# Attention with complex decay and a low-rank mixer on one core: transposed inputs of five pairs by DMA, matmuls of neighbouring chunks joined, a new order

## The chip, the cores and the metric

The kernel runs on one core of a Trainium2 chip. The core has five engines with a queue each: TensorE (PE: matmuls, with the weight loads as PEld), VectorE (DVE), ScalarE (ACT), GpSimd (POOL) and SyncE (SP); the last two issue DMAs here. The metric is device time of one launch in microseconds, the median of several runs. A difference of about 0.2% can be told from none.

## The reference, cut to what matters

B = 4 batches, H = 8 heads, S = 768 tokens, D = 48. Attention is a linear recurrence with a complex gate, whose magnitude is held under 0.999; its real output goes into a mixer over tokens of rank 32 and an MLP over 384 channels. All tensors are f32 for this kernel's purpose, and the order of the sums is free.

```python
mag = np.sqrt(a_re * a_re + a_im * a_im)
scale = np.minimum(mag, 0.999) / (mag + 1e-06)
a_re_n, a_im_n = (a_re * scale, a_im * scale)
for t in range(S):
    new_re = ar * S_re - ai * S_im
    new_im = ar * S_im + ai * S_re
    kv = np.einsum('bhd,bhe->bhde', k[:, :, t], v[:, :, t])
    S_re, S_im = (new_re + kv, new_im)
    y[:, :, t] = np.einsum('bhd,bhde->bhe', q[:, :, t], S_re)
x = attn_out.transpose(0, 2, 1, 3).reshape(B, S, H * D)
u = x + (x.transpose(0, 2, 1) @ U @ V).transpose(0, 2, 1)    # U: 768x32, V: 32x768
out = u + np.maximum(u @ w_ch1, 0.0) @ w_ch2                  # 384x1536, 1536x384
```

## The kernel before

**Chunks.** The 3072 tokens are 24 chunks `i` of 128 (six to a batch), each in two halves of 64. For a chunk, gates are loaded, their magnitudes and angles are summed along the tokens with matmuls against a prefix matrix (L777, L782, L842, L845), and q and k are turned by the gates. q and k are then split into 16-bit halves (ACT, L466), written to DRAM (SP, L933) and read back by a DMA transpose (SP, L934), or transposed on TensorE (L908). `chain(i)` (L938) then does for all heads: the products q*k inside each half (L956, psum "inner"), a masked copy into AT, the state's increments of each half (`state`, L976, into two psum banks `dk`), the states GM and G by additions, what a half adds from inside itself (`inside`, L1005, two psum banks `y`), what comes from before it (`before`, L1013, into the same two banks), and three ScalarE copies out of `y` into `xo` (L1022, L1024).

**Pairs.** `mixer(m)` (L1029) works on pairs of chunks, m = 0 to 11. Once a batch's six chunks are there, `rank` (L1048) forms xU, `spread` (L1071) forms its product with V for each chunk, DVE adds it to `xo` (L472), and `turned` transposes the result: three TensorE transposes a chunk (L1087) into a psum bank and one ScalarE copy to `uT` (L1091). For the first pairs the hidden layer comes from `up` (L1102, L1142) and `down` (L1303); from pair 3 on `up_fewer` makes the first product by a scheme with fewer products: DVE forms twelve combinations of uT's blocks (`put`, L1186), TensorE multiplies them in groups (`few`, L1214, 8 records to a group), ScalarE or a DVE operation makes h, and `down_two` (L1346) forms the second product, which DVE adds to `xo`. The result leaves by DMA from POOL.

**Psum banks.** Kinds "Y" and "T" share five banks, which go round (`psum`): `dk`, `y`, `rank`, `spread`, the transposes, the prefix sums and some of the `few` groups all take the next one. "inner" has its own, `down` and `few` have others.

**Order.** The functions only record operations in a `Plan`, each with its engine, reads, writes and an estimated cost. A table of operation numbers, `ORDER`, sets the sequence in which they are emitted, and so the sequence on every engine's queue; the compiler keeps it. `SPARE` (L1506) and `WARM` (L1513) put idle matmuls at some numbers. `again` (L665) loads the gates once more to find their range and issues one DMA of 192 KB for each chunk and each part (L671).

Of the kernel before, what the change touches and what calls it, by code (L numbers as in the profile page):

```python
# [10 lines left out]
FP = mybir.dt.float32  # L11
I32 = mybir.dt.int32
# [106 lines left out]
)  # L119

SPARE = {
    410: 3, 447: 1,
}

WARM = {
    112: (2, 1), 126: (1,), 136: (2, 2, 2, 2, 2, 2, 1), 141: (2,), 162: (2, 2, 2), 235: (2, 2, 2, 2, 1), 242: (2,), 245: (2,), 259: (2, 2, 1), 266: (1, 1, 1, 1, 1, 1, 1, 1, 1),
}

AIM = {}

DUMP = None

# [194 lines left out]
def kernel(  # L327
# [40 lines left out]
    GROUPS = [(n, n + GC) for n in range(0, NT, GC)]  # L368
    PARTS = [[(n, n + 1) for n in range(GC)]] + [[g] for g in GROUPS[1:]]
    NG = len(GROUPS)  # L370
    AGAIN = range(NG)

    EARLY, SPREAD = 6, (0, 1, 2)
    SPLIT = range(3, NG)
# [563 lines left out]
    def chain(i):  # L938
# [26 lines left out]
        if not last:  # L965
            buffer(G, "G", 2, [DQ, H, D])
# [616 lines left out]
```

## Time and profile before

| | us |
|---|---|
| median of 3 runs | 530.15 (529.94 to 530.81) |
| the profiled execution | 529.77 |
| its span | 528.0 |
| mean granted TensorE clock | 0.997 |
| gate loads on SP, 48 of them `again`'s | 96 of 192.0 KB |
| DMA packets, bytes | 280670, 87.06 MB |

The profile is of one execution. Times of matmuls are of records: a matmul in f32 leaves two records, and a row "x6" of the timeline stands for three matmuls of the code. Records overlap in TensorE's pipeline, so the cost of a group is the distance from its first start to the next group's.

### The profile page before, as it was taken

How to read it: one execution, taken by the hardware profiler on the slowest of the kernel's cores; microseconds unless marked ns; L12 is line 12 of the kernel's file. 1: busy time of each engine (PE TensorE's matmuls, PEld its weight loads, DVE VectorE, ACT ScalarE, POOL GpSimd, SP SyncE). 2: the span in 40 equal slices, each digit the busy share in tenths (PEclk: the TensorE clock that was granted, in tenths of full speed). 3: DMA queues.
4: the chain of work that ended last, by engine and by line, in shares of the span. 5: the costliest groups of instructions: out<-in, count | busy, mean ns of one | idle time of the engine just before them, and what ended most of it. 6: DMA issues, size and time to landing. Idle time of an engine off the chain costs nothing.

```text
span 528.0 us, 15692 instructions
## 1 busy us (share of the span) xinstructions
PE 509.3 (96%) x6670; PEld 460.3 (87%) x6670; DVE 414.5 (79%) x787; ACT 346.0 (66%) x555; POOL 31.6 (6%) x61
## 2 busy tenths in 40 slices
PE   4999999899999999999999999999999999999996
PEld 2777887666998997999999989999999989999996
DVE  4779897799989987898798797878796575958452
ACT  8899998998869978978896768843543313131100
POOL 1000000001010000101011000110000000000110
PEclk9999999999999999999999999999999999999998
DMA  9959958479999998999899958999897543333101
GB/s 226 173 115 270 209 115 191 140 138 217 197 215 244 216 215 145 204 217 202 205 198 227 210 144 175 170 242 229 192 217 178 108 90 61 76 60 61 39 32 35
DMA packets 280670, 87.06 MB, mean 165 GB/s; under 512 B 271288, under 2 KB 272784, under 8 KB 280592
## 3 DMA queue, kind: packets, MB, share of 16 engines
q1 hardware_dynamic: 278384, 81.63, 76.0%
q0 software_dynamic: 2208, 4.35, 2.4%
q8 instruction: 54, 0.88, 0.7%
q14 instruction: 24, 0.20, 0.1%
HBM read 43.03 MB, written 23.63 MB: 126 GB/s over the span
## 4 chain that ended last, share of the span: by engine, by line
PE 88%; ACT 5%; DMA 3%; DVE 2%; issue 1%; SPq 0%; ACTq 0%
PE down L1346 25%; PE few L1214 14%; PE bank L1214 11%; PE up L1102 6%; PE inner L956 4%; PE bank L1013 4%; PE bank L976 4%; PE down L1303 3%; PE bank L1005 2%; DMA gate<-F 2%; PE bank L1071 2%; PE bank L1087 2%; ACT gate L466 1%; PE bank L777 1%; PE bank L782 1%; PE bank L842 1%
## 5 line engine op out<-in xcount | busy, mean ns | idle before, releaser
L466 ACT ACTIVATE gate<-gate 128x768 f32<-128x768 f32 (+2 forms) x85 | 86.1, 1018 | 25.8 <-DMA gate<-in_a_im_dram 14.7
L1346 PE MATMUL down<-w,h 128*128 128x192 f32 x396 | 70.4, 328 | 0.0
L466 ACT ACTIVATE QK<-QKC 128x768 uint16<-128x768 uint16 (+1 forms) x72 | 58.5, 848 | 13.1 <-DVE QKC L469 7.9
L1346 PEld LDWEIGHTS down<-w,h 128*128 128x128 f32 x396 | 64.6, 190 | 1.2 <-issue 0.8
L469 DVE TENSOR_TENSOR QKC<-qk,cs 128x768 f32<-128x768 f32 x48 | 44.9, 952 | 1.0 <-ACT cs L466 0.6
L472 DVE TENSOR_TENSOR xo<-down,xo 128x192 f32<-128x192 f32 (+1 forms) x79 | 29.9, 385 | 14.3 <-PE down L1346 14.1
L1222 ACT COPY h<-few 128x512 f32<-128x512 f32 x35 | 20.2, 583 | 27.8 <-PE few L1214 27.6
L1222 ACT COPY h<-bank 128x512 f32<-128x512 f32 x25 | 14.3, 588 | 36.0 <-PE bank L1214 31.0
L1346 PE MATMUL down<-stage 128*128 128x192 f32 x198 | 37.2, 328 | 0.0
L1102 PE MATMUL up<-uT,w 128*128 128x256 f32 x144 | 33.8, 383 | 0.0
L1346 PEld LDWEIGHTS down<-stage 128*128 128x128 f32 x198 | 32.5, 190 | 0.3 <-issue 0.2
L1102 PEld LDWEIGHTS up<-uT,w 128*128 128x128 f32 x144 | 26.7, 190 | 4.9 <-issue 0.6
L1290 POOL DMA_DIRECT2D out_dram<-xo x32 | 18.5, 590 | 202.9 <-DVE xo L472 164.5
L463 ACT ACT_TABLE_LOAD x22 | 28.2, 1283 | 1.1 <-PEq L1567 0.7
L828 POOL DMA_DIRECT2D gate<-F x15 | 12.0, 797 | 274.7 <-DVE stage L616 86.3
L1226 DVE CUSTOM_DVE_ANT_1 h<-few,h 128x512 f32<-128x512 f32 x31 | 21.0, 686 | 8.8 <-PE few L1214 8.1
L1214 PE MATMUL few<-extra,w 128*128 128x128 f32 x216 | 27.8, 275 | 0.0
L956 PE MATMUL inner<-QK 112*64 112x64 f32 x768 | 27.5, 224 | 0.2 <-DVE AT L959 0.2
L466 ACT ACTIVATE cs<-F 128x384 f32<-128x384 f32 x48 | 24.4, 518 | 3.9 <-DVE F L851 3.7
L956 PEld LDWEIGHTS inner<-QK 112*64 112x64 f32 x768 | 24.5, 138 | 2.4 <-issue 0.8
L1214 PEld LDWEIGHTS few<-extra,w 128*128 128x128 f32 x216 | 26.3, 192 | 0.1
L466 ACT ACTIVATE es<-bank 128x384 f32<-128x384 f32 x44 | 18.4, 502 | 9.2 <-PE bank L777 8.2
(185 smaller groups left out, 1166.8 us busy)
## 6 DMA issues: line engine op xcount, KB each, us to landing
xd<-QK SPq DMA_DIRECT2D x36, 512.0 KB
gate<-in_a_re_dram SPq DMA_DIRECT2D x48, 192.0 KB
gate<-in_a_im_dram SPq DMA_DIRECT2D x48, 192.0 KB
stage<-in_moe_w_ch_dram SPq DMA_DIRECT2D x12, 768.0 KB
qk<-in_q_dram SPq DMA_DIRECT2D x24, 192.0 KB
qk<-in_k_dram SPq DMA_DIRECT2D x24, 192.0 KB
VP<-in_v_dram SPq DMA_DIRECT2D x24, 192.0 KB
out_dram<-xo POOLq DMA_DIRECT2D x12, 192.0 KB, 4.2
```

The lines of the kernel that those rows point to most:

```text
L463: ACT(1.37, rank, lambda: nc.scalar.preload_act_table_set(name), writes=[TABLE])
L466: return nc.scalar.activation(out=o, in_=i, func=f, **kw)
L469: nc.vector.tensor_tensor(out=o, in0=a, in1=b, op=OP.mult)
L472: nc.vector.tensor_tensor(out=o, in0=a, in1=b, op=OP.add)
L956: nc.tensor.matmul(out=get(*ps0)[r:r + HC, h], lhsT=k_of(h, r, HC), rhs=q_of(h, r, HC), start=True, stop=True, tile_position=(0, r))
L976: nc.tensor.matmul(out=get(*dk[r])[x:x + D, h], lhsT=get(*ks)[at, h, x // DP, 0:D], rhs=get(*VPi)[at, h], start=True, stop=True, tile_posi ...
L1013: nc.tensor.matmul(out=get(*y[u])[side(r, u), p], lhsT=q_of(h, r * HC, HC), rhs=get(*(mid_G if r else ("G", i - 1)))[:, h], start=False, s ...
L1102: nc.tensor.matmul(out=get(*ps)[:, e], lhsT=w1[:, f, (ff + e) * 128:(ff + e + 1) * 128], rhs=get(*uT)[:, f], start=(f == 0), stop=(f == KD ...
L1214: nc.tensor.matmul(out=get(*ps)[:, q], lhsT=w()[:, q * 128:(q + 1) * 128], rhs=v[0](), start=(n == 0 and q == 0), stop=True, skip_group_ch ...
L1222: ACT(c_act(n3 * CH) - 0.045, RU, lambda i=i, k=k: nc.scalar.copy(out=at(i, k), in_=get(*ps)), [ps], [o])
L1226: DVE(c_dve(n3 * CH), RU, lambda i=i, k=k: nc.vector._custom_dve(dve_ops.TENSOR_ADD_SAT, out=at(i, k), in0=get(*ps), in1=at(i, k), s0=math ...
L1346: nc.tensor.matmul(out=get(*to)[:, part], lhsT=x(j), rhs=y[:, j], start=(first and j == 0), stop=(j == KH - 1), skip_group_check=not first)
```

## The change

1. For pairs 7 to 11 (`TURNED`) the chunk's input is transposed by DMA: `across` splits the f32 values into 16-bit halves on ScalarE (two instructions, into one tile XU), SP writes them to DRAM (192 KB, tag XV, six buffers) and SP reads them back with a DMA transpose into `uT`. The other pairs keep their TensorE transposes.
2. From chunk 8 on (`JOIN`), except for the first chunk of a batch, the operations of two neighbours are joined: `state` of chunk i (all heads) with `inside` of i-1 as one operation, then the `before`s of i-1 with the products of i as one. The psum banks of i-1's `y` are so taken together with i's `dk`, and the ScalarE copies of i-1 are recorded after the masked copy of i. 14 chunks are joined.
3. `again` loads two chunks of a gate with one DMA, contiguous in memory. The range does not depend on the layout.
4. The transposes take `uT` themselves, where before `spread` depended on it.
5. `ORDER`, `SPARE` and `WARM` are new, made with longer times for instructions. SPARE goes from 4 to 2 matmuls, WARM from 33 to 32 (22 of 256 columns instead of 19, 10 of 128 instead of 14).

The diff without the table of numbers, cut:

```diff
 SPARE = {
-    410: 3, 447: 1,
+    422: 1, 447: 1,
 }
@@
+    JOIN = 8
@@
+    XU = singles.tile([128, 2, DM], U16, name="XU")
@@
+    TURNED = (7, 8, 9, 10, 11)
@@ again
-        for (nm, src), i in ((a, i) for a in ((ar, a_re), (ai, a_im)) for i in range(lo, hi)):
-            SP(c_dma(DM), ("load", 30 + n), lambda nm=nm, src=src, i=i: nc.sync.dma_start(out=get(*nm)[:, i - lo], in_=rows(src, i)),
-               writes=[nm + (i,)])
+        b, c = where(lo)
+        for nm, src in ((ar, a_re), (ai, a_im)):
+            SP(c_dma(W), ("load", 30 + n), lambda nm=nm, src=src: nc.sync.dma_start(
+                out=flat4(nm), in_=src[b, :, c * CH:(c + hi - lo) * CH].rearrange("h t d -> h (t d)").rearrange("h (p m) -> h p m", m=W)), writes=[nm])
@@ chain
+        joined, joins = c > 0 and i >= JOIN, not last and i + 1 >= JOIN
...
+        if joined:
+            p_inside, p_in, p_y, p_befores, p_b, p_leaves, p_rooms, p_takes = pending.pop(i - 1)
+            p_rooms()
+
+            def fused_x():
+                state(0, H)
+                p_inside()
+            PE(1.3, RR, fused_x, [ks, VPi] + p_in, [dk[r] for r in parts_k] + p_y, way=3, steps=4 * H * len(parts_k) + 4 * H,
+               takes=[mid_G] + p_takes)
+            states(True)
+
+            def fused_y():
+                p_befores()
+                products()
+            PE(1.8, RR, fused_y, p_b + [QK], p_y + [ps0], takes=[ATi], way=1, steps=8 * H)
+            states(False)
+            kept()
+            p_leaves()
+        else:
+            PE(0.947, RL, products, [QK], [ps0], takes=[ATi], way=1, steps=4 * H)
+            kept()
+            for h0 in (0, HH):
+                PE(0.443, RR, lambda h0=h0: state(h0), [ks, VPi], [dk[r] + (h0,) for r in parts_k], way=3,
+                   steps=4 * HH * len(parts_k),
+                   takes=[mid_G] + ([] if last else [G]))
+            states(True)
+        if joins:
+            pending[i] = inside, y_in, y, befores, b_in, leaves, rooms, [xi]
+            return
@@ mixer, spread
-            PE(0.76, R0, products, [r, ("V", 0)] + [uT + ("kept",)] * (m >= AHEAD), ps, way=5, steps=8)
+            PE(0.76, R0, products, [r, ("V", 0)], ps, way=5, steps=8)
@@ mixer, turned
+            if m in TURNED:
+                across(cc, i, u)
+                return
...
-            PE(0.33, R0, turn, [u], [tr], steps=KD)
+            PE(0.33, R0, turn, [u], [tr], takes=[uT], steps=KD)
@@
+        def across(cc, i, u):
+            xu, xv = ("xu", i), ("xv", i)
+            ring(xu, "xu", [XU])
+            buffer(xv, "XV", 6, [CH, DM], bass.MemoryType.DRAM)
+            for n in range(2):
+                ACT(c_act(DM), R0, lambda n=n: act(get(*xu)[:, n], get(*u).bitcast(U16).rearrange("p (m n) -> p m n", n=2)[:, :, n], AF.Copy),
+                    [u], [xu + (n,)])
+            SP(0.6, R0, lambda: nc.sync.dma_start(out=get(*xv).bitcast(U16), in_=get(*xu).rearrange("p n m -> p (n m)")), [xu], [xv])
+            SP(0.8, R0, lambda: nc.sync.dma_start_transpose(
+                out=get(*uT).rearrange("p f (c t) -> p f c t", c=MC)[:, :, cc].bitcast(U16),
+                in_=get(*xv).bitcast(U16).rearrange("t (n m) -> (t n) m", n=2)), [xv], [uT + (cc,)])
```

Three places of TensorE's queue. First, `spread` and the transposes of batch 1 (chunks 6 to 11) before, where all of `spread` and two prefix matmuls stand ahead of the transposes:

```order
L1071 MATMUL bank_61<-r,V 128x192
L1071 MATMUL bank_62<-r,V 128x192
L1071 MATMUL bank_61<-r,V 128x192
L1071 MATMUL bank_62<-r,V 128x192
L1071 MATMUL bank_63<-r,V 128x192
L1071 MATMUL bank_64<-r,V 128x192
L1071 MATMUL bank_63<-r,V 128x192
L1071 MATMUL bank_64<-r,V 128x192
L842 MATMUL bank_65<-GS_96,prefix_r 128x384
L842 MATMUL bank_65<-GS_97,prefix_r 128x384
L1087 MATMUL bank_61<-ident,xo 128x128 x3
L1087 MATMUL bank_62<-ident,xo 128x128 x3
```

and now:

```order
L1093 MATMUL bank_63<-xo,UV 32x384 x12
L1116 MATMUL bank_64<-r,V 128x192
L1116 MATMUL bank_65<-r,V 128x192
L1116 MATMUL bank_64<-r,V 128x192
L1116 MATMUL bank_65<-r,V 128x192
L1135 MATMUL bank_61<-ident,xo 128x128 x3
L1135 MATMUL bank_62<-ident,xo 128x128 x3
L1116 MATMUL bank_63<-r,V 128x192
L1116 MATMUL bank_64<-r,V 128x192
L1116 MATMUL bank_63<-r,V 128x192
L1116 MATMUL bank_64<-r,V 128x192
L976 MATMUL bank_65<-VP_118,QKC_106 48x48 x2
```

The transposes of the first pair stand between the two halves of `spread`, right behind the half that they need.

Second, the first join: the end of `state` of chunk 8 and the begin of `inside` of chunk 7, now:

```order
L976 MATMUL bank_62<-VP_120,QKC_108 48x48 x2
L976 MATMUL bank_63<-VP_120,QKC_108 48x48 x2
L976 MATMUL bank_62<-VP_120,QKC_108 48x48 x2
L976 MATMUL bank_63<-VP_120,QKC_108 48x48 x2
L976 MATMUL bank_62<-VP_120,QKC_108 48x48 x2
L976 MATMUL bank_63<-VP_120,QKC_108 48x48 x2
L1000 MATMUL bank_64<-VP_119,AT_123 64x48
L1000 MATMUL bank_65<-VP_119,AT_123 64x48
L1000 MATMUL bank_64<-VP_119,AT_123 64x48
```

(`VP_120` and `QKC_108` are chunk 8's, `VP_119` and `AT_123` chunk 7's.) Before, `inside` and the `before`s of chunk 7 ended ahead of five groups of `down`, and `state` of chunk 8 came behind them:

```order
L1013 MATMUL bank_62<-GM,QK_101 64x48
L1013 MATMUL bank_61<-GM,QK_101 64x48
L1013 MATMUL bank_62<-GM,QK_101 64x48
L1346 MATMUL down<-stage,more 128x192 x3
L1346 MATMUL down<-stage 128x192 x6
L1346 MATMUL down<-w_77,h 128x192 x6
L1346 MATMUL down<-w_77,stage 128x192 x3
L1346 MATMUL down<-w_77,more 128x192 x3
L976 MATMUL bank_63<-VP_119,QKC_107 48x48 x2
L976 MATMUL bank_64<-VP_119,QKC_107 48x48 x2
```

What moved: `inside` of chunk 7 now follows `state` of chunk 8 directly, in two more banks, 64 and 65 beside 62 and 63; before, each pair of banks stood by itself, with `down` in between.

Third, the last batch (chunks 18 to 23). Before, transposes of pair 9 stood between the steps of `down`:

```order
L1346 MATMUL down<-w_77,h 128x192 x3
L1346 MATMUL down<-stage,h 128x192 x3
L1346 MATMUL down<-stage 128x192 x3
L1346 MATMUL down<-stage,h 128x192 x3
L1087 MATMUL bank_61<-ident,xo 128x128 x3
L1346 MATMUL down<-stage,more 128x192 x3
L1087 MATMUL bank_62<-ident,xo 128x128 x3
L1346 MATMUL down<-stage 128x192 x3
L1346 MATMUL down<-w_77,h 128x192 x6
L1214 MATMUL bank_63<-extra,w_76 128x128 x4
```

and now the same place has none; `few` groups stand between the spreads of pairs 9 and 10, and `down` follows:

```order
L1274 MATMUL few<-uT,w_77 128x128 x4
L1274 MATMUL bank_63<-gate,w_77 128x128 x4
L1274 MATMUL few<-extra,w_77 128x128 x4
L1274 MATMUL bank_64<-extra,w_77 128x128 x4
L1274 MATMUL bank_63<-gate,extra 128x128 x4
L1274 MATMUL few<-extra 128x128 x4
L1274 MATMUL few<-gate,w_77 128x128 x4
L1116 MATMUL bank_65<-r,V 128x192
L1116 MATMUL bank_61<-r,V 128x192
L1116 MATMUL bank_65<-r,V 128x192
L1116 MATMUL bank_61<-r,V 128x192
L1116 MATMUL bank_62<-r,V 128x192
```

```order
L1406 MATMUL down<-w_78,h 128x192 x9
L1406 MATMUL down<-stage,h 128x192 x3
L1406 MATMUL down<-w_78,h 128x192 x3
L1406 MATMUL down<-stage,h 128x192 x3
L1406 MATMUL down<-stage 128x192 x3
L1406 MATMUL down<-stage,more 128x192 x3
L1406 MATMUL down<-stage 128x192 x3
L1406 MATMUL down<-w_78,h 128x192 x6
L1274 MATMUL bank_64<-extra,w_77 128x128 x4
```

What moved: the transposes are gone from the queue, and TensorE next touches the transposed input of pair 9 in the `few` groups behind this `down`.

More of the change, by code (lines that the diff above doesn't have):

```diff
@@ L950, in chain @@
         ps0 = ("inner", i)
-        psum(ps0, "A", [128, H, HC])
+        last = c == NCH - 1
+        joined, joins = c > 0 and i >= JOIN, not last and i + 1 >= JOIN
+        G, mid_G = ("G", i), ("GM", i)
+        ks, dk = ("qkc", 2 * i + 1), [("dk", (i, r)) for r in range(2)]
+        parts_k = range(1 if last else 2)
+        y, xi = [("y", (i, r)) for r in range(2)], ("xo", i)
+        y_in = [VPi, ATi, mid_G] + ([("G", i - 1)] if c else [])
         def products():
@@ L957, in products, with kept, state @@
                                      tile_position=(0, r))
-        PE(0.947, RL, products, [QK], [ps0], takes=[ATi], way=1, steps=4 * H)
-        DVE(0.17 + 0.00104 * H * HC, RL, lambda: nc.vector.copy_predicated(
-            out=get(*ATi), mask=mask.bitcast(I32).unsqueeze(1).to_broadcast([128, H, HC]), data=get(*ps0)), [ps0, ("mask", 0)], [ATi])
-        G, mid_G, last = ("G", i), ("GM", i), c == NCH - 1
-        ks, dk = ("qkc", 2 * i + 1), [("dk", (i, r)) for r in range(2)]
-        buffer(mid_G, "GM", 2, [DQ, H, D])
-        if not last:
-            buffer(G, "G", 2, [DQ, H, D])
-        parts_k = range(1 if last else 2)
-        for r in parts_k:
-            psum(dk[r], "Y", [128, H, D], [128, H, DP])
-        def state(h0):
-            for h in range(h0, h0 + HH):
+        def kept():
+            DVE(0.17 + 0.00104 * H * HC, RL, lambda: nc.vector.copy_predicated(
+                out=get(*ATi), mask=mask.bitcast(I32).unsqueeze(1).to_broadcast([128, H, HC]), data=get(*ps0)), [ps0, ("mask", 0)], [ATi])
+        def state(h0, n=HH):
+            for h in range(h0, h0 + n):
                 for r in parts_k:
@@ L977, in state, with states @@
                                          start=True, stop=True, tile_position=(r * HC, x))
-        for h0 in (0, HH):
-            PE(0.443, RR, lambda h0=h0: state(h0), [ks, VPi], [dk[r] + (h0,) for r in parts_k], way=3,
-               steps=4 * HH * len(parts_k),
-               takes=[mid_G] + ([] if last else [G]))
         half0, half1 = (lambda r=r: get(*dk[r])[0:DQ] for r in range(2))
-        if c:
-            DVE(c_dve(DM), RR, lambda: add(get(*mid_G), get("G", i - 1), half0()), [("G", i - 1), dk[0]], [mid_G])
-        else:
-            ACT(c_act(DM), RR, lambda: nc.scalar.copy(out=get(*mid_G), in_=half0()), [dk[0]], [mid_G])
-        if not last:
-            DVE(c_dve(DM), RR, lambda: add(get(*G), get(*mid_G), half1()), [mid_G, dk[1]], [G])
-            DVE(c_dve(DM), RR, lambda: mul(get(*G), get(*G), T_of(i)), [("T", group_of(i))], [G])
-        y, xi = [("y", (i, r)) for r in range(2)], ("xo", i)
-        for r in range(2):
-            psum(y[r], "Y", [128, HH, D], [128, HH, CH])
-        buffer(xi, "xo", 8, [128, DM])
+        def states(first):
+            if not first:
+                pass
+            elif c:
+                DVE(c_dve(DM), RR, lambda: add(get(*mid_G), get("G", i - 1), half0()), [("G", i - 1), dk[0]], [mid_G])
+            else:
+                ACT(c_act(DM), RR, lambda: nc.scalar.copy(out=get(*mid_G), in_=half0()), [dk[0]], [mid_G])
+            if not last and first != joined:
+                DVE(c_dve(DM), RR, lambda: add(get(*G), get(*mid_G), half1()), [mid_G, dk[1]], [G])
+                DVE(c_dve(DM), RR, lambda: mul(get(*G), get(*G), T_of(i)), [("T", group_of(i))], [G])
         def side(r, u):
@@ L1015, in before, with befores, rooms, halves @@
                                      tile_position=(0, (r ^ u) * HC), skip_group_check=True)
-        PE(0.44, RR, inside, [VPi, ATi, mid_G] + ([("G", i - 1)] if c else []), y, way=3, takes=[xi], steps=4 * H)
+        def befores():
+            for r in range(0 if c else 1, 2):
+                before(r)
+        def rooms():
+            for r in range(2):
+                psum(y[r], "Y", [128, HH, D], [128, HH, CH])
+            buffer(xi, "xo", 8, [128, DM])
+        def halves(a):
+            return a.rearrange("p (a u d) -> p a u d", u=2, d=D)
@@ new lines, in leaves @@
+        def leaves():
+            ACT(c_act(HH * D) - 0.04, RR, lambda: nc.scalar.copy(out=halves(get(*xi))[:, :, 0], in_=get(*y[0])), [y[0]], [xi + (0,)])
+            for r in range(2):
+                ACT(c_act(HH * D) + 0.04, RR, lambda r=r: nc.scalar.copy(out=halves(get(*xi))[r * HC:(r + 1) * HC, :, 1],
+                                                                         in_=get(*y[1])[side(r, 1)]), [y[1] + (r,)], [xi + (r + 1,)])
+        b_in = [QK, mid_G] + ([("G", i - 1)] if c else [])
@@ new lines, in chain @@
+        psum(ps0, "A", [128, H, HC])
+        buffer(mid_G, "GM", 2, [DQ, H, D])
+        if not last:
+            buffer(G, "G", 2, [DQ, H, D])
+        for r in parts_k:
+            psum(dk[r], "Y", [128, H, D], [128, H, DP])
+        if joined:
[14 more added lines that the diff above has]
+            p_leaves()
+        else:
+            PE(0.947, RL, products, [QK], [ps0], takes=[ATi], way=1, steps=4 * H)
[5 more added lines that the diff above has]
+            states(True)
@@ L1017, in chain @@
+        if joins:
+            pending[i] = inside, y_in, y, befores, b_in, leaves, rooms, [xi]
+            return
+        rooms()
+        PE(0.44, RR, inside, y_in, y, way=3, takes=[xi], steps=4 * H)
         if c:
```

12 lines of the change are left out of this document (4 added, 8 removed), and 172 rows, old and new, of the table ORDER.

## The prediction

> **What bounds the kernel now.** I read the page first (busy shares, the 40 slices, the chain of waits), then the waits of TensorE's queue, then the table of windows, then the timeline of TensorE at the places that the change touches.
>
> ```profile
> PE 509.3 (96%) x6670; PEld 460.3 (87%) x6670; DVE 414.5 (79%) x787; ACT 346.0 (66%) x555; POOL 31.6 (6%) x61
> PE   4999999899999999999999999999999999999996
> ACT  8899998998869978978896768843543313131100
> PE 88%; ACT 5%; DMA 3%; DVE 2%; issue 1%; SPq 0%; ACTq 0%
> 160.00:290.00 130.00, 128.25 (x1960) 121.71 (x1958) 114.29 (x221) 110.87 (x170) 10.94 (x17) 1.00 1.01 207
> 290.00:410.00 120.00, 120.00 (x1800) 115.52 (x1797) 98.21 (x192) 70.83 (x122) 8.19 (x13) 1.00 0.96 195
> ```
>
> The last two rows are windows: stretch, its length, then PE, PEld, DVE, ACT and POOL busy with their counts, granted clock, DMA share, GB/s. TensorE is busy 96% of the span, 88% of the chain is its own work, and from 290 to 410 us it never rests (120.00 of 120). So a microsecond of TensorE work taken out is worth a microsecond, until something else comes late; ScalarE has room only in the second half (slices of 1 to 5 tenths), and DMA is full until 410 us (1.01, 0.96).
>
> Where TensorE did rest, its waits say for whom:
>
> ```profile
> PE bank L782 <- DVE GL L742: 7.7, 1, 7.7
> PE up L1142 <- ACT more L1128: 2.1, 1, 2.1
> PE down L1346 <- DVE xo L472: 1.1, 1, 1.1
> PE bank L1071 <- ACT r L1054: 0.6, 1, 0.6
> PE bank L976 <- issue: 0.4, 1, 0.4
> 151.00 6.34 DMA gate<-F
> 275.81 6.09 DMA gate<-F
> ```
>
> 7.7 us lie at the start, which the change does not touch. The rest is about 4 us, and some of that hangs on small loads from POOL's queue (the two rows of the chain, each 6 us long).
>
> **The change part by part.**
>
> *Transposes.* Ten chunks (pairs 7 to 11) lose three TensorE transposes and one copy each.
>
> ```profile
> L1087 PE MATMUL bank<-ident,xo 128*128 128x128 f32 x72 | 11.9, 281 | 0.0
> 430.65 1.14 PE L1346 MATMUL down<-stage,h 128*128 128x192 f32 x6
> 431.63 0.49 PE L1087 MATMUL bank<-ident,xo 128*128 128x128 f32 x3
> 431.96 1.14 PE L1346 MATMUL down<-stage,more 128*128 128x192 f32 x6
> L1091 ACT COPY uT<-bank 128x384 f32<-128x384 f32 x21 | 9.6, 476 | 16.3 <-PE bank L1087 16.3
> ```
>
> Durations overlap in the pipeline, so I price by starts: the step after three transposes starts 431.96 - 431.63 = 0.33 us later. Ten times 0.33 is **-3.3 us** of TensorE. Were the mean of 281 ns the price, 30 would cost 8.4; the starts exclude that.
>
> [...]
>
> *What stands in their place.* Per chunk: two ACT splits of 384 elements, a write of 192 KB from SP to DRAM, a DMA transpose from SP. Nearest rows:
>
> ```profile
> L466 ACT ACTIVATE QK<-QKC 128x768 uint16<-128x768 uint16 (+1 forms) x72 | 58.5, 848 | 13.1 <-DVE QKC L469 7.9 <-DMA xd<-QK 5.2
> L934 SPq DMA_TRANSPOSE QK<-xd x36: 1732/2794/4559, 119.3 to 407.5; - x36
> out_dram<-xo POOLq DMA_DIRECT2D x12, 192.0 KB, 4.2
> DMA to landing us min/median/max: 1.9/3.5/6.1
> ```
>
> The two splits cost at least 0.85 together (848 ns is for 768 elements, twice as many as one has) and at most 1.7; I take 0.95, since the 384-element copy above takes 476. The write lands in 1.9 to 6.1 (all stores of the output: least, median, most); I take 4.2, the row of the same size. The transpose holds SP for 1.05 (2.79 x 3/8, by bytes) to 4.56, and I let it land 4 us after its issue. XU is a single tile, so the second chunk's splits wait for the first write. A pair so takes 0.95 + 4.2 + 0.95 + 4.2 + 1.5 + 4 = about 16 us, where it took some 1.2; with every upper bound 1.7 + 6.1 + 1.7 + 6.1 + 4.56 + 6.1 = 26, with the lower ones 0.85 + 1.9 + 0.85 + 1.9 + 1.05 + 1.9 = 8.5. The cover is what TensorE has between a pair's `spread` and its first `few`:
>
> ```profile
> 426.12 1.57 PE L1071 MATMUL bank<-r,V 64*128 64x192 f32 x16
> 427.62 1.24 PE L1346 MATMUL down<-w,h 128*128 128x192 f32 x6
> 412.71 1.06 PE L1214 MATMUL bank<-gate,extra 128*128 128x128 f32 x8
> 413.60 1.06 PE L1214 MATMUL few<-uT,w 128*128 128x128 f32 x8
> 414.59 1.15 PE L956 MATMUL inner<-QK 112*64 112x64 f32 x32
> ```
>
> `spread` is 1.50 for two pairs, a `few` group of 8 records 0.89, six `down` records 431.63 - 430.65 = 0.98. The tightest is pair 9 in the last batch: seven `few` groups, two spreads and 66 `down` records follow its own spread, 7 x 0.89 + 1.50 + 11 x 0.98 = **18.5 us**; by the same counting pairs 7, 8, 10 and 11 have 28 to 65. 18.5 against 16 hides it: **0**, but with 2.5 to spare, and 7.5 short at the upper bounds. ScalarE pays ten times 0.95 - 0.48, 5 us in stretches where it is under half busy: 0.
>
> *Joins.* For 14 chunks state(i) and inside(i-1) stand together, and befores(i-1) and products(i).
>
> ```profile
> 40.59 0.94 PE L976 MATMUL bank<-VP,QKC 64*48 64x48 f32 x64
> 41.34 0.65 PE L1005 MATMUL bank<-VP,AT 64*64 64x48 f32 x32
> 161.46 0.94 PE L976 MATMUL bank<-VP,QKC 64*48 64x48 f32 x64
> 162.33 1.15 PE L956 MATMUL inner<-QK 112*64 112x64 f32 x32
> 400.59 0.64 PE L1013 MATMUL bank<-GM,QK 112*64 112x48 f32 x16
> 401.05 1.12 PE L956 MATMUL inner<-QK 112*64 112x64 f32 x32
> 419.27 0.64 PE L1013 MATMUL bank<-G,QK 112*64 112x48 f32 x16
> 419.84 1.16 PE L1214 MATMUL few<-extra 128*128 128x128 f32 x8
> ```
>
> State takes 0.75 ahead of inside and 0.87 ahead of products; a `before` 0.46 ahead of products and 0.57 ahead of full-size work. The order makes 12 new neighbours of the first kind and 7 of the second (8 stood so already): 12 x 0.12 + 7 x 0.11 = 2.2. Against that, the new order turns from full-size to small tiles 60 times instead of 51, and each turn costs the 0.10 by which 413.60 to 414.59 exceeds 412.71 to 413.60, with 0.1 more on the way back: 9 x 0.2 = 1.8. So **-0.4 us**, between +0.5 and -2.2. The join gathers little because the order gathered before.
>
> *Waits it adds.* A join holds two `dk` and two `y` banks, four of the five that all of "Y" and "T" share, and the copies of i-1 come after kept(i). What releases banks:
>
> ```profile
> L1024 ACT COPY xo<-bank 64x192 f32<-64x192 f32 x48 | 14.9, 313 | 9.5 <-PE bank L1013 8.7
> 206.22 2.14 PE L1048 MATMUL bank<-xo,UV 128*32 128x384 f32 x24
> 208.96 1.57 PE L1071 MATMUL bank<-r,V 64*128 64x192 f32 x16 [0.60 <-ACT r L1054]
> 210.46 0.62 PE L842 MATMUL bank<-GS,prefix_r 128*128 128x384 f32 x2
> 435.61 0.55 DVE L472 TENSOR_TENSOR xo<-bank,xo 128x384 f32<-128x384 f32 x1
> ```
>
> At the first join nothing stands ahead of the fourth bank but the last copies: 2 of 0.31, **+0.65**, between 0 and three copies (0.94). Elsewhere `few` groups stand between and I take 0 (the rival below takes more). In batch 1 the transposes now follow the first half of `spread` at once; before, its other half and two L842 matmuls lay between. A transpose needs the DVE addition of its chunk, 0.55 and about 0.2 to hand over: **+0.75**, between 0 and 210.92 - 208.96, some 2.0. Behind that wait stand the other spreads and state of chunk 12.
>
> *Loads and fillers.* 48 gate loads become 24 of twice the size, same bytes; 24 issues less on SP, 0 on the path. Idle and warm matmuls: one 256-wide group of three more, four 128-wide less, about 0.
>
> Sum: 529.77 (this execution; its span is 528.0) - 3.3 - 0.4 + 0.65 + 0.75 = 527.5; the median shown, 530.15, stands 0.38 higher, so **527.8**. With the bounds (-2.2 or +0.5; 0 or 2.9 for the waits) 524.7 to 530.2, and its own range, leaving out that all bounds meet, 525.6 to 529.4.
>
> **The rivals.**
>
> 1. *The turn by DMA comes late: slower.* If a pair's chain passes 18.5 us at pair 9, DVE's first `put` stands at the head of its queue for uT; behind it stand the additions that free the two `down` banks, and TensorE stops at `down` and `few`. It decides from 2.5 us more than my 16. For it: SP is one queue in order, the transposes of q and k take 4.56 at worst, and xv writes wait there for ACT; pair 8 lies where DMA is still full. Against: DMA is a third full after 410 us. At the upper bounds 7.5 late once: 527.8 + 7.5 = 535; halfway, and with a part given back behind the wait, **532.5**.
>
> 2. *The joins wait each time: no change.* 14 joins with 0.2 for the copies (two thirds of one) are 2.8: **530.4**. For it: four of five banks. Against: the rows of `few` between most joins.
>
> 3. *Better.* The order was made anew with longer times for instructions; if the 1.1 and 0.4 and the 2.1 of the waits above go too: 527.8 - 2.8 = **525.0**. Against: those hang on DMA and ScalarE, which the change gives more to do.
>
> 4. *A transpose costs its full record:* 30 x 0.281 instead of 3.3, 5.1 more off, **522.7**. The starts speak against it.
>
> [...]
>
> 5. *The joins do nothing they say* is in the forecast's bounds (-0.4 to +0.5).
>
> **How the numbers follow.** Forecast 0.41, rival 1 0.34, rival 2 0.14, rival 3 0.09, rival 4 0.02. About 0.2% (1.06 us) either way is what can be told here. Faster: 0.39 of the forecast's 0.41, and rivals 3 and 4, 0.50; within 0.2%: rival 2 and the forecast's 0.02, 0.16; slower 0.34. The range must take in most of rivals 1 and 3: 524.3 to 533.5 leaves out the late end of rival 1 (0.1), rival 4 and a part of 3 (0.05).
>
> **What would show it.** L1135 with 42 records and 7 us in the groups; TensorE's waits: a transpose at some 211 us waiting for DVE's addition by about 0.75, the first inside of a join for ACT's xo by 0.65, and neither `few` nor `down` waiting after 290 us. Rival 1 shows as DVE waiting for DMA uT with TensorE idle behind it between 300 and 520; rival 2 as fourteen small idles ahead of L976 or L1000. The forecast is wrong if TensorE's busy time falls by less than 3 or its idle grows by more than 3 us.

## The result, and the profile after

The changed kernel takes 547.93 us (median of 5 runs, 547.2 to 550.85) against 530.15: 1.035 times as long, 95% interval 1.0319 to 1.038. The profiled execution is the slowest of the five (550.85 us); it spans 549.0 us, where the kernel before had 528.0. From the page of the changed kernel, the busy shares and TensorE in 40 slices:

```profile
PE 516.0 (94%) x6634; PEld 462.0 (84%) x6634; DVE 415.5 (76%) x787; ACT 352.4 (64%) x565; POOL 31.5 (6%) x61
PE   4999999999999998999999999997899699899996
```

TensorE's idle time rose from 528.0 - 509.3 = 18.7 to 549.0 - 516.0 = 33.0 us, and its busy time by 6.7, although it has fewer matmuls. The granted clock accounts for most of the second: 0.986 over 549.0 us leaves 7.7 us of full clock missing, 0.997 over 528.0 leaves 1.6; the difference is 6.1 (an estimate from these figures). The row of slices shows where time went: up to the 27th it is about as full as before, then there are holes where before there was none. The windows of that stretch (PE, PEld, DVE, ACT, POOL busy, granted clock, DMA share, GB/s), first of the kernel before, then of the changed one:

```profile
380.00:400.00 20.00, 20.00 (x297) 19.60 (x295) 17.31 (x37) 6.86 (x13) 1.62 (x3) 1.00 0.97 207
420.00:440.00 20.00, 20.00 (x154) 17.89 (x155) 12.42 (x28) 5.62 (x13) 0.54 (x1) 1.00 0.44 80
```

```profile
380.00:400.00 20.00, 14.40 (x142) 14.03 (x141) 11.13 (x20) 9.04 (x16) 0.00 (x0) 0.83 0.98 190
420.00:440.00 20.00, 14.98 (x219) 12.45 (x216) 8.61 (x16) 7.37 (x16) 0.00 (x0) 0.96 0.35 96
```

5.6 and 5.0 us of idle time in two windows, and a granted clock of 0.83 in the first. Who is waited for stands in TensorE's waits of the changed kernel (us in total, times, longest):

```profile
PE bank L1274 <- ACT h L1282: 5.7, 3, 3.0
PE few L1274 <- ACT h L1282: 5.6, 1, 5.6
PE few L1274 <- DVE h L471: 1.4, 1, 1.4
PE bank L1116 <- ACT r L1099: 0.9, 1, 0.9
...
PE bank L1135 <- DVE xo L471: 0.7, 1, 0.7
```

TensorE waits for ScalarE to copy `h` out of psum: the first two rows make 11.3 of the 14.3 us by which its idle time grew, and the kernel before has no such row. But ScalarE is busy 64% of the time; so the question is what ScalarE waits for. First its longest DMA wait before, then after:

```profile
ACT gate L466 <- DMA gate<-in_a_im_dram: 14.7, 5, 7.0
```

```profile
ACT gate L465 <- DMA gate<-in_a_im_dram: 45.6, 9, 8.9
```

That is the load of `again`. One stall in full, from the timelines of SP, ScalarE and TensorE of the changed kernel (start, us, engine, line):

```profile
370.88 5.17 SPq L936 DMA_TRANSPOSE QK<-xd  x1
376.10 0.65 SPq L674 DMA_DIRECT2D gate<-in_a_im_dram  x1
```

```profile
374.74 0.32 ACT L1027 COPY xo<-bank 64x192 f32<-64x192 f32 x1
383.62 0.84 ACT L465 ACTIVATE gate<-gate 128x768 f32<-128x768 f32 x1 [8.57 <-DMA gate<-in_a_im_dram]
384.49 0.58 ACT L1282 COPY h<-bank 128x512 f32<-128x512 f32 x1
...
385.49 0.57 ACT L1282 COPY h<-few 128x512 f32<-128x512 f32 x1
```

```profile
379.36 1.16 PE L1274 MATMUL few<-extra,gate 128*128 128x128 f32 x8
386.12 2.08 PE L1274 MATMUL few<-extra,w 128*128 128x128 f32 x8 [5.60 <-ACT h L1282]
387.99 1.91 PE L1274 MATMUL bank<-gate,extra 128*128 128x128 f32 x8
389.69 1.55 PE L1274 MATMUL few<-uT,w 128*128 128x128 f32 x8
391.18 0.67 PE L1008 MATMUL bank<-G,QK 112*64 112x48 f32 x16
```

SP issues the load at 376.10, behind a transpose that held its queue for 5 us. ScalarE has stood at the square of that load since 375.06 and starts it at 383.62; behind it in the queue stand the two copies of `h` at 384.49 and 385.49; TensorE, which has run out at about 380.5, goes on at 386.12. Then it pays a second time: the next 8 records take 387.99 - 386.12 = 1.87 us instead of 0.89, with a granted clock of 0.50 from 385 to 390 us (shown at the end).

How the load itself runs is seen late in the kernel, where little else is in flight. DMA's busy share in 40 slices of 430.6 to 436.5 us of the changed kernel, which one pair of joined loads (256 packets of 3072 bytes) fills, with one write of 192 KB to XV beginning in it:

```profile
DMA  4860442354545547263564446488997544644445
```

Mostly four to six tenths: the packets of the queue take 55.4% of the time of 16 DMA engines in this window. The same pair as four loads of 192 KB in packets of 192 bytes, 429.5 to 433.9 us of the kernel before, with a store of 96 KB beside it:

```profile
DMA  0388999999999998899999999999999999985994
```

By their packets' starts, first to last, the pairs whose loads are issued one right behind the other (the last six before, the last eight now) take 4.1 to 4.9 us before and 5.1 to 6.4 us now; counted at the start of each packet, in the median 9 joined packets are in flight. `again`'s joined load has the 8 heads as its outermost dimension. The cost that the code records for such a load is 768 * 512 / 250e3 = 1.57 us, 3.1 for the pair. The table `ORDER` was made with longer times for instructions; whether the load's was longer too is not on record.

### The profile page after: what moved, and what is told of

Same layout as the page of the kernel before. It is cut to its first block, busy times and chain, and to the rows that moved or that the text cites. A ratio compares the mean times of both kernels' runs of the same rounds, so it can differ in the third digit from the quotient of the medians.

```text
span 549.0 us, 15605 instructions
## 1 busy us (share of the span) xinstructions
PE 516.0 (94%) x6634; PEld 462.0 (84%) x6634; DVE 415.5 (76%) x787; ACT 352.4 (64%) x565; POOL 31.5 (6%) x61
## 2 busy tenths in 40 slices
DMA packets 243453, 90.98 MB, mean 166 GB/s; under 512 B 229720, under 2 KB 232496, under 8 KB 243376
## 5 line engine op out<-in xcount | busy, mean ns | idle before, releaser
L465 ACT ACTIVATE gate<-gate 128x768 f32<-128x768 f32 (+2 forms) x85 | 86.0, 1016 | 55.1 <-DMA gate<-in_a_im_dram 45.6
L1162 PE MATMUL up<-uT,w 128*128 128x256 f32 x144 | 35.2, 394 | 0.2 <-ACT uT L1139 0.2
L1282 ACT COPY h<-bank 128x512 f32<-128x512 f32 x25 | 14.3, 581 | 31.6 <-PE bank L1274 31.5
L1274 PE MATMUL few<-extra,w 128*128 128x128 f32 x216 | 29.2, 283 | 5.6 <-ACT h L1282 5.6
L1162 PEld LDWEIGHTS up<-uT,w 128*128 128x128 f32 x144 | 27.6, 197 | 5.4 <-issue 1.2
L976 PEld LDWEIGHTS bank<-VP,QKC 64*48 64x48 f32 x1408 | 19.9, 121 | 5.9 <-issue 2.5
```

The costliest lines, as they stand in the source:

```text
L465: return nc.scalar.activation(out=o, in_=i, func=f, **kw)
L976: nc.tensor.matmul(out=get(*dk[r])[x:x + D, h], lhsT=get(*ks)[at, h, x // DP, 0:D], rhs=get(*VPi)[at, h], start=True, stop=True, tile_posi ...
L1162: nc.tensor.matmul(out=get(*ps)[:, e], lhsT=w1[:, f, (ff + e) * 128:(ff + e + 1) * 128], rhs=get(*uT)[:, f], start=(f == 0), stop=(f == KD ...
L1274: nc.tensor.matmul(out=get(*ps)[:, q], lhsT=w()[:, q * 128:(q + 1) * 128], rhs=v[0](), start=(n == 0 and q == 0), stop=True, skip_group_ch ...
L1282: ACT(c_act(n3 * CH) - 0.045, RU, lambda i=i, k=k: nc.scalar.copy(out=at(i, k), in_=get(*ps)), [ps], [o])
```

## The experiments

All ratios are to the kernel before, run beside them (530.4 to 530.6 us).

### Loads in the old form, in the changed kernel

```diff
-        for nm, src in ((ar, a_re), (ai, a_im)):
-            SP(c_dma(W), ("load", 30 + n), lambda nm=nm, src=src: nc.sync.dma_start(
-                out=flat4(nm), in_=src[b, :, c * CH:(c + hi - lo) * CH]...rearrange("h (p m) -> h p m", m=W)), writes=[nm])
+        def both(nm, src):
+            for i in range(lo, hi):
+                nc.sync.dma_start(out=get(*nm)[:, i - lo], in_=rows(src, i))
+        for nm, src in ((ar, a_re), (ai, a_im)):
+            SP(c_dma(W), ("load", 30 + n), lambda nm=nm, src=src: both(nm, src), writes=[nm])
```

> The changed kernel with its gate loads of `again` in the old form (two DMAs of 192 KB in runs of 192 bytes, issued one behind the other), all else and the order as changed. Theory A (the joined load is the cause: in the trace of the changed kernel only 8 or 9 of its packets of 3072 bytes are in flight at once, so a pair of loads lands some 7.4 us after its issue, ScalarE waits 45.6 us for in_a_im at the head of its queue, and the copies of h that TensorE waits for stand behind it): 529 to 537 us, and ScalarE's waits for in_a_im fall to 15 to 25 us. Theory B (the transposes by DMA and the new order make SP late, whatever the form of the load): 543 to 550, waits for in_a_im still over 35.

Measured: 539.75 us, ratio 1.0146 (1.0106 to 1.0185). A pair takes 4.2 to 5.5 us. ScalarE's wait fell, but not as far as in the kernel before:

```profile
ACT gate L465 <- DMA gate<-in_a_im_dram: 27.6, 9, 5.7
```

It lies between the ranges of both theories, and the wait is over the 15 to 25 of theory A: the form of the load is worth 8 us, and that is not all.

### The joined load over 16

```diff
-                ...rearrange("h (p m) -> h p m", m=W)), writes=[nm])
+                ...rearrange("h (p m) -> p h m", m=W)), writes=[nm])
```

> The changed kernel with the joined load of `again` kept, but its partitions in the other order (the 16 parts of a head outermost, the 8 heads inside; the range that is formed does not depend on it), all else as changed. Theory A, in the form that the outer dimension of 8 limits the packets in flight: 16 in flight, the pair lands in some 4 us, time 526 to 534. If the size of the packets were the limit and not their spread: no change, 545 to 550. Theory B: 543 to 550.

Measured: 534.0 us, ratio 1.0062 (1.0035 to 1.0088): 13.9 of the 17.8 us lost are back, with the same bytes, packets, queue and order. DMA's share in 429.7 to 433.2 us, one pair:

```profile
DMA  0999949946347899979897989896979798998999
```

Mostly nine tenths, 16 or 17 packets in flight, a pair in 3.2 to 3.9 us. Not the size of the packets (256 of 3072 bytes a pair in both) but the dimension that stands outermost had set the time here: 9 packets were in flight with 8 outermost, 16 or 17 with 16. By the queue's line of the two windows, in which some packets of XV's writes and transposes are counted as well, it is 55.4% and 105.9% of 16 engines' time, 8.9 and 16.9 packets in the mean. By what mechanism the outermost dimension sets this was not shown.

ScalarE's wait for the load is no shorter than with the old form (27.6), although the kernel takes 5.75 us less:

```profile
ACT gate L465 <- DMA gate<-in_a_im_dram: 27.7, 8, 6.4
```

So ScalarE's total does not give the time. TensorE's longest wait for `h`, with the old form (of this the profile shows the slowest execution of four, 543.59 us) and with 16 outermost, does fall:

```profile
PE few L1276 <- ACT h L1284: 3.0, 1, 3.0
```

```profile
PE few L1274 <- ACT h L1282: 1.8, 1, 1.8
```

And so do VectorE's waits for the load and its square (L661 and L662 together): 24.5 us in the changed kernel, 12.9 with the old form, 6.2 with 16 outermost. How much of the loss runs over ScalarE and how much over VectorE, these runs do not separate.

### Both forms of the joined load in the kernel before

```diff
-        for (nm, src), i in ((a, i) for a in ((ar, a_re), (ai, a_im)) for i in range(lo, hi)):
-            SP(c_dma(DM), ..., lambda ...: nc.sync.dma_start(out=get(*nm)[:, i - lo], in_=rows(src, i)), writes=[nm + (i,)])
+        def load(nm, src):
+            if nm not in loaded:
+                loaded.add(nm)
+                nc.sync.dma_start(out=flat4(nm), in_=src[b, :, c * CH:(c + hi - lo) * CH]...rearrange("h (p m) -> h p m", m=W))
+        for (nm, src), i in ((a, i) for a in ((ar, a_re), (ai, a_im)) for i in range(lo, hi)):
+            SP(c_dma(DM), ..., lambda nm=nm, src=src: load(nm, src), writes=[nm + (i,)])
```

The second kernel has "p h m" in place of "h p m".

> The kernel before with nothing but the joined load of `again` (heads outermost), in its own order; the joined load stands where the first of the two stood. Theory A: slower, 534 to 542, ScalarE's waits for in_a_im from 15 up to 30 or more. Theory B: 529 to 532.

> The kernel before with the joined load in the other order of partitions (16 outermost). Theory A: no slower than before, 528 to 531. Theory B: the same, 529 to 532; together with the run of heads outermost it tells whether the spread of the load counts by itself.

Measured: heads outermost 531.95 us, ratio 1.0031 (1.0011 to 1.0051); 16 outermost 530.91, ratio 1.001 (0.9991 to 1.0029). The first is a miss for theory A, which had 534 to 542: the pairs take 5.0 to 6.1 us there too, and it costs 1.5 us. ScalarE's waits with heads outermost (with 16 they are 10.4, in 5):

```profile
ACT gate L466 <- DMA gate<-in_a_im_dram: 19.9, 7, 6.6
```

So the load alone is not the cause either. It is the slow load in the new order: in the old one ScalarE waits less for the same load (19.9 against 45.6), and TensorE has no wait for `h` at all, with either form. What in the old order gives the room was not tried by a run. One difference is in SP's waits: in the kernel before, the load stands at the head of SP's queue until the range step frees its buffer, and so is issued as early as it can be; in the changed kernel this wait is 0.7 us in one place.

```profile
SPq L671 <- DVE low L661: 48.6, 10, 9.2
```

### More idle matmuls at the early correction

```diff
-    422: 1, 447: 1,
+    422: 3, 447: 1,
```

> The changed kernel with the joined load spread over 16 (534.0 us) and SPARE 422 at 3 idle matmuls instead of 1, as many as the kernel before had at that place. Theory C (early loss: at 108.5 us TensorE idles 0.51 ahead of a correction, and its granted clock then falls to 0.75 from 110 to 115 us; twelve records of `up` take 4.38 us at 108.79 where they took 2.59 before; the two idle matmuls left out had kept it busy): 531.5 to 533 us, no slice under 0.95 between 105 and 120. Rival: the wait is for a result, not for work, and more idle matmuls only lengthen the queue: 534 to 535.

Measured: 533.91 us, ratio 1.0074 (1.0039 to 1.0109), no different from 534.0. Rows of the windows with granted clock, first without, then with:

```profile
110.00:115.00 5.00, 4.72 (x21) 3.19 (x20) 1.67 (x4) 2.89 (x6) 0.77 (x1) 0.75 1.07 175
```

```profile
110.00:115.00 5.00, 4.49 (x27) 2.98 (x26) 3.35 (x9) 4.60 (x8) 0.77 (x1) 1.00 0.89 134
```

The granted clock is full in that profile, but it shows one execution of four: the profiled one (532.83 us) has a mean clock of 0.999, the others 0.993 to 0.996 and 533.79 to 536.8 us. Without the added matmuls the six executions have 0.993 to 0.999 and 532.2 to 536.0 us. So in both the executions at 0.999 are the shortest, and the added matmuls were not seen to raise the clock of all: the run does not test what the dip costs.

### The square by GpSimd

```diff
-        ACT(c_act(W), R1, lambda: act(flat4(ai), flat4(ai), AF.Square), [], [ai])
+        POOL(c_act(W), R1, lambda: nc.gpsimd.tensor_tensor(out=flat4(ai), in0=flat4(ai), in1=flat4(ai), op=OP.mult), [], [ai])
```

> The changed kernel, loads as changed (heads outermost, two take 5 to 6 us), with one difference: the square of a_im in `again` is made by GpSimd instead of ScalarE, so that ScalarE's queue no longer stands behind the load. Theory A in the form that the place of the wait decides (ScalarE's h copies stand behind the square): 532 to 540 us, ScalarE's waits for in_a_im gone, TensorE's waits for h on ScalarE under 2 us. Rival: VectorE, which forms the range behind the same load, is then the queue that stands: 542 to 549, with VectorE's waits for in_a_re and the square up to some 40 us.

Measured: 548.66 us, ratio 1.0357 (1.0309 to 1.0404): the rival's range. Waits of VectorE, first in the changed kernel, then here, and then of TensorE here:

```profile
DVE low L662 <- ACT gate L465: 15.3, 7, 5.8
```

```profile
DVE low L662 <- POOL gate L676: 14.8, 6, 3.6
DVE gate L661 <- DMA gate<-in_a_re_dram: 7.7, 5, 2.3
```

```profile
PE bank L976 <- DVE GM L471: 2.6, 1, 2.6
PE bank L1274 <- DVE h L471: 1.9, 1, 1.9
```

ScalarE's waits for the load are down to 0.3 us, and TensorE's for ScalarE's `h` from 11.3 to 2.5. VectorE stands at the range steps as long as in the changed kernel, 22.5 us where the rival had up to 40, and behind them are GM and the `h` that VectorE makes. The square itself takes 1.46 us on GpSimd, 0.84 on ScalarE, so the run also makes the steps behind it later.

### The turn by TensorE

```diff
-            ring(xu, "xu", [XU])
-            buffer(xv, "XV", 6, [CH, DM], bass.MemoryType.DRAM)
-            for n in range(2):
-                ACT(c_act(DM), R0, lambda n=n: act(get(*xu)[:, n], ...
-            SP(0.6, R0, lambda: nc.sync.dma_start(out=get(*xv)...
-            SP(0.8, R0, lambda: nc.sync.dma_start_transpose(...
+            tr = out_of("uTp", i, [128, KD, CH], [128, 4, CH])
+            PE(0.33, R0, turn, [u], [tr], takes=[uT], steps=KD)
+            ACT(c_act(DM) - 0.045, R0, lambda: nc.scalar.copy(out=get(*uT)[:, :, cc * CH:(cc + 1) * CH], in_=get(*tr)), [tr], [uT + (cc,)])
+            for n in range(2):
+                SP(0.6, R0, lambda: None, [uT + (cc,)], [])
```

An operation whose inputs or psum bank are not free at its place stands a little later; the order is otherwise kept.

> The changed kernel with the joined load spread over 16 (534.0 us), without the transposes by DMA: TensorE's transposes and ScalarE's copy stand where the two splits stood, the two SP steps emit nothing. If the turn by DMA is hidden and saves TensorE's 30 records (3.3 to 3.6 us by the starts): 536.5 to 539. Theory B (the turn costs more on SP and ScalarE than it saves): 530 to 533.

> The changed kernel, loads as changed (heads outermost), without the transposes by DMA, as in the run beside it. Theory A (the loads alone make ScalarE late): 547 to 553, no better than the changed kernel. Theory B (SP is late because of the turn's writes and transposes): 533 to 541.

Measured: 545.15 us, ratio 1.0287 (1.0246 to 1.0329), with the load over 16, 11.2 more than with the turn by DMA; and 556.82, ratio 1.0503 (1.0461 to 1.0544), with the loads as changed, 8.9 more. Both lie above every range. Theory B falls twice: in this order the turn by TensorE costs more than the turn by DMA. 11.2 is more than the 30 records: by the profiles TensorE's idle time is 5.8 us longer and its busy time 5.3. The transposes stand where only splits stood, and TensorE waits there for their input:

```profile
PE bank L1165 <- DVE h L1302: 2.5, 1, 2.5
PE bank L1165 <- DVE xo L488: 1.4, 1, 1.4
```

### The readers of the load later

```diff
-        for n in ORDER if ORDER else range(len(self.ops)):
+        for m in sorted(ORDER, key=lambda n, at={n: k for k, n in enumerate(ORDER)}: at[n] + (25.5 if n in self.shift else 0)):
```

`shift` holds the square and the two range steps of `again`. What is not ready at its place waits for it, as above. The second kernel has it with the load over 16 and three idle matmuls.

> The changed kernel, loads as changed (heads outermost), with one difference in the order: the square of a_im and the two range steps of `again` stand 25 places later in the table (loads that wait for a buffer of theirs move behind them; TensorE's rows are the same). Theory A in its last form (the order puts these steps where a load of 3 us would be there, and the load takes 5 to 6; what stands behind them on ScalarE and VectorE, the h that TensorE needs, then waits): 530 to 538 us, ScalarE's waits for in_a_im under 15 us, TensorE's waits for h under 2. Rival (the load itself, through DMA or SP, sets the time wherever its readers stand): 543 to 549.

> All that helped together: the joined load spread over 16, SPARE 422 at 3, the square and range steps 25 places later. If nothing else of the order costs: 530 less the transposes' 3.6, 526 to 528.5. If the rest of the new order (its first 120 us, and the neighbours that it lost) costs 2 to 3 us: 529 to 532. If the steps were no hindrance any more once the load is quick: 533.5 to 534.5, as without them.

Measured: 574.6 us, ratio 1.0831 (1.0765 to 1.0897), and 564.37, ratio 1.0622 (1.0549 to 1.0695). Both far outside every range. From the first of the two, waits of SP, of TensorE and of VectorE:

```profile
SPq L691 <- DVE low L679: 27.2, 5, 8.9
```

```profile
PE inner L983 <- DMA QK<-xd: 9.5, 2, 7.3
PE down L1425 <- DVE xo L488: 6.7, 3, 5.1
```

```profile
DVE gate L1265 <- DMA uT<-xv: 11.7, 2, 7.6
```

ScalarE's waits for the load are still 30.8, where theory A had under 15. The range step frees the buffer that the next load is written to. When it comes later, the load stands at the head of SP's queue, and behind it stand the transposes of q and k and of the mixer's input, for which TensorE and VectorE then wait. The wait at SP's head is not harmful by itself: the kernel before has 48.6 us of it. So in this order the readers can't simply be moved away from a slow load: early, they block ScalarE and VectorE; late, the load blocks SP.

### The loads from GpSimd's queue

```diff
-            SP(c_dma(W), ("load", 30 + n), lambda nm=nm, src=src: nc.sync.dma_start(
+            POOL(c_dma(W), ("load", 30 + n), lambda nm=nm, src=src: nc.gpsimd.dma_start(
```

> The changed kernel with the joined load spread over 16 and SPARE 422 at 3 (533.9 us), and the loads of `again` issued by GpSimd's queue instead of SP's, at the same places of the order. If SP's queue is what makes things late (a load that waits there for VectorE or ScalarE to free its buffer holds up the transposes of q and k and of the mixer's input; with the steps 25 places later that was seen as 27 to 29 us of SP's waits and 7 us of TensorE's): 526 to 531. If SP has enough room once the load is quick: 533 to 535. If the loads take longer from this queue: over 536.

Measured: 539.51 us, ratio 1.0168 (1.0121 to 1.0214), 5.6 more than the same from SP, and in the last range. The page shows the time from issue to landing:

```profile
gate<-in_a_re_dram POOLq DMA_DIRECT2D x12, 384.0 KB, 5.5
```

From SP the profile has only two landings of this load, 5.7 and 6.8 us, so that it takes longer from GpSimd is not shown. Giving SP's queue this room did not help; why the kernel became slower stays open.

### Loads of an eighth

```diff
-                out=flat4(nm), in_=src[b, ...]...rearrange("h (p m) -> h p m", m=W)), writes=[nm])
+                out=flat4(nm)[:, 0:W // 8], in_=src[b, ...]...rearrange("h (p m) -> h p m", m=W)[:, :, 0:W // 8]), writes=[nm])
...
-        ranged(R1, lambda: flat4(ar), lambda: flat4(ar), lambda: flat4(ai), lo, W, [], [ar], [ai])
+        ranged(R1, lambda: flat4(ar), lambda: flat4(ar), lambda: flat4(ai), lo, W, [], [ar], [ai], beside)
```

> The changed kernel with loads of `again` of an eighth of the size, heads outermost as changed; the range steps run over what the rest of their buffers hold and their verdict goes to a tile that nothing reads. Left out: the second look at the gates' range, all but an eighth of its input and its result. If the time that a load takes is the whole of what the changed kernel loses: 526 to 530 (530 less the transposes' 3.6, and the range steps as before). If the rest of the new order costs 3 us beside it, as the load spread over 16 left: 531 to 534. If the wait is for SP's place and not for the load: 540 to 548.

Measured: 530.91 us, ratio 0.9994 (0.997 to 1.0018). A pair's packets take 1.3 to 1.8 us with 8 outermost still. ScalarE's waits for it:

```profile
ACT gate L465 <- DMA gate<-in_a_im_dram: 13.1, 6, 6.3
```

It lies between the first two expectations: 17.0 of 17.8 us hang on the load. The run takes 8.3 MB off the DMA engines as well (82.72 of 90.98 MB are left), so that other transfers may be quicker too; the run in which nothing but the length of the load changes is the one with 16 outermost, with 13.9 us. And even with a load that costs next to nothing the changed kernel is no faster than the one before.

The runs side by side, by the time of a pair (its first packet's start to its last's):

| pair, us | in the changed kernel, us | in the kernel before, us |
|---|---|---|
| 1.3 to 1.8 (an eighth) | 530.91 | |
| 3.1 to 3.9 (16 outermost) | 534.0 | 530.91 |
| 4.1 to 5.5 (old form) | 539.75 | 530.5 |
| 5.0 to 6.4 (8 outermost) | 547.93 | 531.95 |

The column on the right moves by 1.5 us, the other by 17: the new order has little slack for this load, and the old one has.

## Why the prediction was wrong

**The step that failed is "Loads and fillers": "48 gate loads become 24 of twice the size, same bytes; 24 issues less on SP, 0 on the path."** Bytes and issues were counted, the shape was not. With the heads outermost 9 packets of the load were in flight in the median, a pair takes 5.0 to 6.4 us instead of 4.1 to 4.9, and the cost recorded for it is 3.1. In the new order that is worth 13.9 us (16 outermost), 17.0 with nearly the whole load gone, where 0 was taken. No rival named it: rival 1 had a late DMA at the head of a queue, with a like consequence (TensorE stops at `few`) and the wrong DMA; the queues that stood were ScalarE's and VectorE's, at the load of `again`. That 0.34 was given to a slower kernel is no merit of the mechanism. Of the signs of being wrong both came: busy time rose by 6.7 and idle time by 14.3.

**Transposes, -3.3: right.** By the starts, waits apart, the 72 records of before take 8.8 us and the 42 of the changed kernel 5.2: -3.6. A transpose leaves one record here (24 chunks of three make the 72). The mean record is still 281 ns, and 30 of these would have been 8.4; the starts deny that as a price.

```profile
L1135 PE MATMUL bank<-ident,xo 128*128 128x128 f32 x42 | 6.8, 281 | 0.7 <-DVE xo L471 0.7
```

**The turn by DMA, 0: right in that it is hidden.** In the changed kernel neither VectorE nor TensorE has a wait for uT's transpose; it is issued in the median 1.275 us, where 1.5 was taken. Rival 1, with 0.34, did not occur; waits on uT of over 1 us appear only in the two runs with the readers later. Whether the turn's steps on SP make the loads behind them later (they wait there for xv for 16.9 us) no run separates, since the turn by TensorE also moves TensorE's work.

```profile
L1151 SPq DMA_TRANSPOSE uT<-xv x10: 1207/1275/4617, 353.0 to 489.9; - x10
```

**Joins, -0.4: of the other sign.** By the starts of the kernel with 16 outermost, every idle stretch apart, state takes 0.8 us less than before, the products 0.5 and `inside` 0.1 more, `before` the same: -0.1. But the 1200 records of `few` take 137.8 us where they took 135.5, 2.4 more: 28 of them need over 0.15 us to the next of `few` instead of 0.11, where 9 did before, and 17 of the 28 (8 of the 9) are the first behind another kind of operation. Together +2.3, where the bounds were -2.2 to +0.5. The gain of state ahead of inside is there; the turns between kinds of tiles cost more than was counted. Why the other 11 take longer is not shown.

**Waits, +1.4: right in part.** The transposes of batch 1 wait 0.7 for VectorE's addition (0.75 was taken), `spread` 0.9 for r where it was 0.6. Both stand in the list of TensorE's waits at the top. The 0.65 at the first join did not come where it was expected: `inside` of chunk 7 follows state without a wait. Its `before` waits 0.9, and the profile names nobody that it waits for; that of a later join waits 0.4 for ScalarE's xo. The 2.1, 1.1 and 0.4 that rival 3 let go are gone, but other losses outweigh them.

**The sum.** -3.3, -0.4 and +1.4 would have given 527.8. With the load all but taken away it is 530.9, so 3 us more were lost elsewhere in the new order. The profile of that run spans 0.8 us more than the one of before; by the starts that is -3.6 for the transposes, -0.1 for the four parts of the joins, +2.0 for `few`, +1.6 for `up`, +0.7 of idle time and +0.2 for the rest. The loss in `up` is early, where nothing of pairs 7 to 11 runs yet. The correction and `up`, before and in the kernel with 16 outermost:

```profile
108.61 2.75 PE L1102 MATMUL up<-uT,w 128*128 128x256 f32 x12
111.20 0.49 PE L1087 MATMUL bank<-ident,xo 128*128 128x128 f32 x3
```

```profile
108.47 0.49 PE L1566 MATMUL up<-ident 128*128 128x128 f32 x2 [0.51 <-DVE extra L1208]
108.79 4.44 PE L1162 MATMUL up<-uT,w 128*128 128x256 f32 x12
113.17 0.92 PE L1116 MATMUL bank<-r,V 64*128 64x192 f32 x8
115.23 0.49 PE L1562 MATMUL down<-ident 128*128 128x128 f32 x2 [0.51 <-DVE extra L1208]
```

Twelve records take 4.38 us instead of 2.59, with two waits of 0.51 around them; the granted clock of 110 to 115 us is 0.75, as shown above. What brings the clock down there was not shown, and it does not fall in every execution: with loads of an eighth, the three at a mean clock of 0.999 or 1.0 take 528.1 to 529.6 us and the six at 0.990 to 0.996 take 530.4 to 532.5.

No version was found that beats the kernel before; the nearest are the kernel before with the joined load over 16 (ratio 1.001) and the changed kernel with loads of an eighth (0.9994), which leaves work out.

## What to carry to other kernels

Price a joined or reshaped DMA anew: with the same bytes and packets the joined load took 5.0 to 6.4 us a pair with 8 outermost and 3.1 to 3.9 with 16, so look at which dimension stands outermost and count the packets in flight, not the bytes. The order here put readers close behind a load that took 5.0 to 6.4 us where 3.1 was recorded; three queues (the load's, and its two readers') handed the lateness on, and moving the readers only chose which of them stands. Try such a part in the old order as well: that it costs 1.5 us there and 13.9 in the new one tells that neither the part nor the order alone sets the price.

## What the runs showed of the hardware

With 8 outermost a pair of loads of 128 packets of 3072 bytes each kept 9 packets in flight, with 16 outermost 16 or 17; a pair took 5.0 to 6.4 against 3.1 to 3.9 us, also against 4.1 to 4.9 for sixteen times as many packets of 192 bytes. And the stall of TensorE shown first was followed by slower records: after 5.60 us of idle time the granted clock was 0.50 from 385 to 390 us, and the next 24 records took 391.18 - 386.12 = 5.06 us; three groups at 0.89 are 2.7. That the stall is what lowers the clock was not shown by a run. The windows around it:

```profile
380.00:385.00 5.00, 0.52 (x5) 0.33 (x3) 0.50 (x1) 1.35 (x3) 0.00 (x0) 0.89 1.04 170
385.00:390.00 5.00, 3.88 (x18) 3.89 (x19) 3.06 (x6) 3.95 (x9) 0.00 (x0) 0.50 0.86 193
```
